# Key and query norms by crossbar DMA and GpSimd sums, shifts of two slots in one instruction, and 32 more score blocks on VectorE, in a one-core attention and GLU kernel

## The chip, the cores and the metric

The kernel runs on one core of one Trainium2 chip. The metric is the device time of one execution in microseconds (us), as a median of several executions. All executions here are of one core, so "state" only means that a run was not more than 1.5% above the fastest of the same kernel; all runs quoted are in the fast state. Beside the time, each run has the mean granted clock of TensorE (1.0 is full speed).

## The reference

A gate mixes an attention block of 32 heads of 16 numbers with a gated linear unit, for 2048 tokens of 512 numbers, all in bf16:

```python
qkv = (x @ wqkv).reshape(B, S, 3, H, Dh).transpose(2, 0, 3, 1, 4)   # S 2048, H 32, Dh 16
q, k, v = qkv[0], qkv[1], qkv[2]
scores = einsum("bhqd,bhkd->bhqk", q, k) * Dh ** -0.5
a = einsum("bhqk,bhkd->bhqd", softmax(scores), v).transpose(...).reshape(B, S, D) @ wo
h = sigmoid(x @ w_gate) * (x @ w_up)          # 512 -> 1792
b = h @ w_down
g = sigmoid((x * gate_w).sum(-1))
out = g * a + (1 - g) * b
```

Every head has 16 x 4 score blocks of 128 keys by 512 queries, 2048 blocks in all, and each of their 134 million scores has to be exponentiated. That is the work that counts here.

## The kernel before

The kernel is a planner and a player. A list of tasks, each with an engine, an expected duration, what it depends on and the buffers it holds, is put in order by a simulated run of the engines; then every engine plays its list. Instructions on an engine run strictly in that order. The numbers of the plan (priorities, and per unit of four heads a set of "knobs") are tuned to the kernel.

The exponentials are shared out. ScalarE takes most blocks, two or three to an instruction. VectorE takes some by integer arithmetic on the bits of an fp16 number: one pass from PSUM makes a block of bits, and two shifted copies (shifts by a constant, within SBUF) are weighted together afterwards by the value matmuls, so such a block costs three value matmuls instead of one. `D_HALVES` says how many pairs of blocks of each of the 32 units go to VectorE; the sum is 267.

```python
# a pair of blocks on VectorE: the pass from PSUM is make_x; two shifts, m = 1 and 2, of 128x1024
for m in range(1, NPH):
    x = P.add("dve", 0.36, lambda v, bp=bp, m=m: v.tensor_scalar(
        PDu[:, bp.slot, m, :, :], PDu[:, bp.slot, 0, :, :], float(PH_OFF[m]), None, op0=ALU.add), [], [bp], kind="x", prio=PH_PRIO)
# blocks on ScalarE, two or three in one instruction
e = P.add("act", 0.175 + 0.3665 * len(ts), lambda a: a.activation(some(PA, out), some(ps_all, bs), ACTF.Exp, bias=ACT_BIAS, scale=SCALE), ...)
```

The softmax is made safe by a bound: minus half the squared norm of each query and minus half the largest squared norm of a key are put into two spare rows of the 32-row score matmul. The norms are made like this for three of the four groups of eight heads and for 15 of the 16 query blocks:

```python
# key_proj(g, c), g > 0: a key block of 128 rows (8 heads) by 512 keys
ev = dve.tensor_copy(kraw, bk(b))                                # from PSUM
s  = pool.tensor_tensor(ksq, kraw, kraw, ALU.mult)               # squares, GpSimd
...                                                              # two masks of the keys, GpSimd tensor_scalar
last = P.group(..., full(b2, wn, ksq))                           # sums of 16 rows: a matmul on TensorE
eNK[g, c] = dve.tensor_reduce(am[:, g, c:c + 1], bk(b2), AX.X, ALU.min)    # VectorE, from PSUM
# query(c, g)
ev = dve.tensor_copy(Q[:, slot, 0, :], bk(b))
s  = pool.tensor_tensor(qsq, Q0, Q0, ALU.mult);  cp = pool.tensor_copy(Q1, Q0)
l2 = P.group(..., full(b2, wn, qsq))                             # TensorE
en = dve.tensor_scalar(nsb, bk(b2), a_[:, g:g + 1], None, op0=ALU.add)     # VectorE, from PSUM
for r in range(2): dma("sp", Q[o:128:32, slot, r, :], nsb[o:128:32, :], ...)
```

## Time and profile before

Median 755.75 us in the three runs taken first (755.69 to 756.17), with the clock at 0.999 in the profiled run.

The table of stretches gives one line for a stretch: its bounds, its length, then the busy us (and count of instructions) of TensorE, of its weight loads, of VectorE, of ScalarE and of GpSimd, then the granted clock, the DMA share and the GB/s.

### The profile page before, as it was taken

How to read it: one execution, taken by the hardware profiler on the slowest of the kernel's cores; microseconds unless marked ns; L12 is line 12 of the kernel's file. 1: busy time of each engine (PE TensorE's matmuls, PEld its weight loads, DVE VectorE, ACT ScalarE, POOL GpSimd, SP SyncE). 2: the span in 40 equal slices, each digit the busy share in tenths (PEclk: the TensorE clock that was granted, in tenths of full speed). 3: DMA queues.
4: the chain of work that ended last, by engine and by line, in shares of the span. 5: the costliest groups of instructions: out<-in, count | busy, mean ns of one | idle time of the engine just before them, and what ended most of it. 6: DMA issues, size and time to landing. Idle time of an engine off the chain costs nothing.

```text
span 754.4 us, 21827 instructions
## 1 busy us (share of the span) xinstructions
PE 739.0 (98%) x9617; PEld 218.0 (29%) x9617; DVE 663.1 (88%) x1311; ACT 734.7 (97%) x822; POOL 111.4 (15%) x198
## 2 busy tenths in 40 slices
PE   8999999999999999999999999999999999999997
PEld 5233232332222222222222222222222222222222
DVE  4999999999898988778899888998889888978986
ACT  5999999999999999999999999999999999999994
POOL 4532625420100101001010010101001000000000
PEclk9999999999999999999999999999999999999999
DMA  9300000040000000000010000000000010000000
GB/s 299 121 10 9 16 4 16 9 115 9 8 9 9 16 16 22 23 2 16 9 17 9 9 23 17 22 9 17 9 1 16 16 23 23 9 10 8 15 2 30
DMA packets 34839, 19.22 MB, mean 25 GB/s; under 512 B 26688, under 2 KB 32696, under 8 KB 34744
## 3 DMA queue, kind: packets, MB, share of 16 engines
q1 hardware_dynamic: 33352, 16.38, 8.4%
q8 instruction: 75, 1.23, 0.7%
q10 hardware_dynamic: 1392, 1.44, 0.6%
q14 instruction: 20, 0.16, 0.1%
HBM read 9.70 MB, written 2.10 MB: 16 GB/s over the span
## 4 chain that ended last, share of the span: by engine, by line
ACT 75%; PE 19%; DVE 4%; DMA 1%; ACTq 0%; issue 0%; DVEq 0%
ACT PA L920 72%; PE ps_all L746 7%; PE ps_all L946 6%; PE ps_all L955 5%; ACT tT L904 3%; DVE PD L928 1%; DVE PD L984 1%; DMA PD<-in_A_x_dram 1%; PE ps_all L749 1%; PE ps_all L866 0%; DVE un L779 0%; DVE am L792 0%; PE ps_all L729 0%; DVE ost L1077 0%; ACTq L635 0%; DVE Q L830 0%
## 5 line engine op out<-in xcount | busy, mean ns | idle before, releaser
L920 ACT ACTIVATE PA<-ps_all 128x1024 bf16<-128x1024 f32 (+1 forms) x744 | 710.5, 1177 | 0.9 <-PE ps_all L946 0.5
L928 DVE TENSOR_SCALAR PD<-ps_all 128x512 uint16<-128x512 f32 x534 | 357.2, 685 | 59.8 <-PE ps_all L946 43.4
L946 PE MATMUL ps_all<-Q,K 32*128 32x512 bf16 x2048 | 301.5, 384 | 6.1 <-ACT PA L920 4.6
L955 PE MATMUL ps_all<-PA,V 128*17 128x512 bf16 x1514 | 242.3, 382 | 1.0 <-ACT PA L920 0.7
L984 DVE TENSOR_SCALAR PD<-PD 128x1024 uint16<-128x1024 uint16 x534 | 216.9, 438 | 4.2
L955 PE MATMUL ps_all<-PD,Vm 128*17 128x512 f16 x1068 | 189.9, 381 | 0.2 <-DVE PD L984 0.2
L946 PEld LDWEIGHTS ps_all<-Q,K 32*128 32x128 bf16 x2048 | 75.0, 91 | 303.5 <-ACT PA L920 272.5
L955 PE MATMUL ps_all<-PD,V 128*17 128x512 f16 x534 | 146.3, 382 | 0.0
L746 PE MATMUL ps_all<-xT,wg 128*32 128x512 bf16 x896 | 74.5, 384 | 0.0
L955 PEld LDWEIGHTS ps_all<-PA,V 128*17 128x17 bf16 x1514 | 55.9, 88 | 55.5 <-issue 43.2
L746 PE MATMUL ps_all<-un,hT 128*32 128x512 bf16 x896 | 71.7, 383 | 0.0
L746 PE MATMUL ps_all<-xT,wu 128*32 128x512 bf16 x896 | 70.0, 383 | 0.1
L1022 POOL TENSOR_TENSOR rs<-rec,e 128x16 f32<-128x16 f32 x32 | 8.3, 259 | 407.3 <-DVE rec L1020 407.3
L955 PEld LDWEIGHTS ps_all<-PD,Vm 128*17 128x17 bf16 x1068 | 44.2, 88 | 34.3 <-issue 26.2
L907 DVE SCALAR_TENSOR_TENSOR hT<-tT,ps_all 128x512 bf16<-128x512 bf16 x56 | 38.1, 680 | 8.6 <-PE ps_all L746 7.6
L904 ACT ACTIVATE tT<-ps_all 128x512 bf16<-128x512 f32 x56 | 42.7, 762 | 0.0
L831 POOL TENSOR_TENSOR qsq<-Q 128x512 bf16<-128x512 bf16 x15 | 16.0, 1069 | 159.7 <-DVE Q L830 159.7
L955 PEld LDWEIGHTS ps_all<-PD,V 128*17 128x17 bf16 x534 | 33.6, 88 | 18.5 <-issue 14.9
L784 POOL TENSOR_SCALAR K<-un,msk 128x512 bf16<-128x512 bf16 x28 | 26.6, 954 | 8.6 <-DVE un L771 5.8
L746 PEld LDWEIGHTS ps_all<-xT,wu 128*32 128x32 bf16 x896 | 19.7, 95 | 26.2 <-issue 13.6
L746 PEld LDWEIGHTS ps_all<-xT,wg 128*32 128x32 bf16 x896 | 17.8, 94 | 26.1 <-issue 20.4
L746 PEld LDWEIGHTS ps_all<-un,hT 128*32 128x32 bf16 x896 | 17.6, 94 | 24.3 <-issue 19.0
(92 smaller groups left out, 331.6 us busy)
## 6 DMA issues: line engine op xcount, KB each, us to landing
wg<-in_B_w_gate_dram SPq DMA_DIRECT2D x1, 1792.0 KB, 11.0
wu<-in_B_w_up_dram SPq DMA_DIRECT2D x1, 1792.0 KB, 14.4
un<-in_B_w_down_dram SPq DMA_DIRECT2D x1, 1792.0 KB, 8.2
out_dram<-ost SPq DMA_DIRECT2D x14, 128.0 KB, 1.8
PD<-in_A_x_dram SPq DMA_DIRECT2D x4, 256.0 KB, 5.6
PD<-in_A_x_dram ACTq DMA_DIRECT2D x4, 256.0 KB, 6.8
un<-in_A_wqkv_dram SPq DMA_DIRECT2D x2, 384.0 KB, 8.8
mid<-mid SPq DMA_TRANSPOSE x45, 2.4
```

The lines of the kernel that those rows point to most:

```text
L746: i = pe.matmul(bk(b)[32 * j:32 * j + 32, :], w()[:, 32 * j:32 * j + 32], x(), start=first, stop=last, tile_position=(0, 32 * j), skip_gro ...
L749: return (MM, lambda pe: pe.matmul(bk(b), w(), x(), start=first, stop=last), four)
L784: eK[g, r, c] = P.add("pool", 1.0, lambda p, r=r: p.tensor_scalar(K[:, g, r, c * 512:(c + 1) * 512], kraw[:, kr.slot, :], msk[:, r:r + 1], ...
L831: s = P.add("pool", 1.15, lambda p: p.tensor_tensor(qsq[:, sq.slot, :], Q[:, bq.slot, 0, :], Q[:, bq.slot, 0, :], ALU.mult), [ev], [sq, bq ...
L904: et = P.add("act", 0.48, lambda a: a.activation(tT[:, t_.slot, :], bk(b), ACTF.Tanh, scale=0.5), [l1], [b, t_], kind="m")
L907: e_h[c, ft] = P.add("dve", 0.62, lambda v: v.scalar_tensor_tensor(hT[:, h_.slot, :], tT[:, t_.slot, :], 1.0, bk(b2), ALU.add, ALU.mult), ...
L920: e = P.add("act", 0.175 + 0.3665 * len(ts), lambda a: a.activation(some(PA, out), some(ps_all, bs), ACTF.Exp, bias=ACT_BIAS, scale=SCALE) ...
L928: return P.add("dve", 0.076 + 0.534 * len(ds), lambda v: v.tensor_scalar(PDu[:, bp.slot, 0, i:i + len(ds), :], some(ps_all, bs), EXP_A, EX ...
L946: return pe.matmul(bk(b), K[32 * j:32 * j + 32, g, r, kt * 128:(kt + 1) * 128], Q[32 * j:32 * j + 32, bq.slot, r, :], start=True, stop=Tru ...
L955: return pe.matmul(bk(bpv)[32 * j:32 * j + DH + 1, :], lhs(h), rhs(), start=t.first, stop=t.last, tile_position=(0, 32 * j), skip_group_ch ...
L984: x = P.add("dve", 0.36, lambda v, bp=bp, m=m: v.tensor_scalar(PDu[:, bp.slot, m, :, :], PDu[:, bp.slot, 0, :, :], float(PH_OFF[m]), None, ...
L1022: e2_ = P.add("pool", 0.2, lambda p: p.tensor_tensor(r4(rs), r4(rec), e2[:, 4 * c:4 * c + 4][:, :, None].to_broadcast([128, 4, 4]), ALU.mu ...
```

## The change

The intent is to take work off ScalarE, the engine that most of the chain consists of, and give it to VectorE, which gets room by losing the norms. Four parts:

1. Norms: each block is transposed by a DMA, squared on GpSimd as before, and summed over its 16 numbers by four GpSimd additions of 256, 128, 64 and 32 columns. Queries are then scaled on GpSimd and transposed back. The norm matmul on TensorE and the VectorE instruction from PSUM go; for keys some small VectorE instructions on 128x32 come.
2. Shifts: when two shifts by the same constant are ready together, one instruction of 128x2048 does both.
3. Blocks: `D_HALVES` sums to 283, so 32 more blocks go from ScalarE to VectorE. A fourth buffer for VectorE's blocks.
4. The plan: a look-ahead to the next unit's value matmuls, new knobs, and more waits between instructions of one engine, with fewer semaphores for DMAs.

```diff
-D_HALVES = (8, 8, 8, 8, 9, 6, 10, 8, 8, 9, 8, 9, 7, 8, 8, 9, 9, 8, 9, 9, 9, 8, 9, 9, 7, 8, 8, 9, 8, 9, 9, 8)
+D_HALVES = (9, 9, 8, 8, 10, 6, 10, 9, 8, 9, 10, 10, 7, 8, 8, 10, 10, 10, 10, 9, 10, 8, 10, 9, 7, 8, 8, 9, 9, 10, 9, 8)
 ... (priorities and knobs: cut)
+        if t.kind == "x" and t.sets:
+            o = next((x for x in self.ready[e] if x.kind == "x" and x.sets and x.n == t.n), None)
+            if o is not None:
+                self.ready[e].remove(o)
+                self._absorb(t, o)
 ... (look-ahead to the next unit's value matmuls: cut)
-        if d.eng == t.eng:
-            if t.eng in ("pe", "sp") or not raw:
+        if d.eng == t.eng:
+            if t.eng in ("pe", "sp"):
                 return
 ...
+    def head_sums(src, deps, bufs):
+        s = Buf(pmid)
+        d = dma_t(lambda: mdt(s), src, deps, bufs + [s])
+        e = pl(1.07, lambda g: g.tensor_tensor(md(s), md(s), md(s), ALU.mult), [d], prio=0.5, bufs=[s])
+        v = lambda: md(s).rearrange("p (x d) -> p x d", d=16)
+        for n in (8, 4, 2, 1):
+            e = pl(0.22 + 0.054 * n, lambda g, n=n: g.tensor_tensor(v()[:, :, 0:n], v()[:, :, 0:n], v()[:, :, n:2 * n], ALU.add), [e],
+                   prio=0.5, bufs=[s])
+        return s, d, e, lambda: v()[:, :, 0]
 ... (keys)
-            s = P.add("pool", 1.15, lambda p: p.tensor_tensor(ksq[:, sq.slot, :], kraw[...], kraw[...], ALU.mult), ...)
+            s, d, e, sums = head_sums(lambda: kraw[:, kr.slot, :], [ev], [kr])
+            if c == 0: eNK[g] = small(lambda v: v.tensor_copy(km[:, :], sums()), ...)
+            else:      eNK[g] = small(lambda v: v.tensor_tensor(km[:, :], km[:, :], sums(), ALU.max), ...)
+            if c == 3: ... (two more maxima, one transpose back, one reduce, one scaling by -0.5)
 ... (queries)
-        l2 = P.group(key - 8.0, [full(b2, lambda: wn[:, :], lambda: qsq[:, sq.slot, :], True, True)], ...)
-        en = P.add("dve", 0.68, lambda v: v.tensor_scalar(nsb[:, ns.slot, :], bk(b2), a_[:, g:g + 1], None, op0=ALU.add), ...)
+        s, d, e, _ = head_sums(lambda: Q[:, bq.slot, 0, :], [ev], [bq])
+        d2 = dma_t(lambda: mdt(s2), lambda: md(s), [e], [s, s2])
+        en = pl(0.95, lambda p: p.tensor_scalar(md(s2), md(s2), -0.5, a2[:, g:g + 1], op0=ALU.mult, op1=ALU.add), ...)
```

## The prediction

> **What bounds the kernel now.** I read the page's engine shares first, then the 40 slices, then the chain that ended last, the groups of instructions, and the waits of ScalarE. From the page (busy time and share of the span; busy tenths per slice; the shares of the chain):
>
> ```profile
> PE 739.0 (98%) x9617; PEld 218.0 (29%) x9617; DVE 663.1 (88%) x1311; ACT 734.7 (97%) x822; POOL 111.4 (15%) x198
> ...
> DVE  4999999999898988778899888998889888978986
> ACT  5999999999999999999999999999999999999994
> POOL 4532625420100101001010010101001000000000
> ...
> ACT 75%; PE 19%; DVE 4%; DMA 1%; ACTq 0%; issue 0%; DVEq 0%
> ```
>
> ScalarE has no open slice between the first and the last, and three quarters of the chain is ScalarE. VectorE has gaps everywhere except in the first third. GpSimd is nearly idle after it. The table of stretches around those borders:
>
> ```profile
> 0.00:20.00 20.00, 17.54 (x161) 10.82 (x161) 10.40 (x27) 11.75 (x20) 10.08 (x35) 1.00 0.95 306
> 20.00:742.00 722.00, 713.28 (x9318) 203.54 (x9316) 646.70 (x1275) 721.11 (x801) 101.06 (x163) 1.00 0.07 17
> 742.00:754.40 12.40, 8.20 (x142) 3.62 (x140) 6.04 (x12) 1.83 (x3) 0.22 (x1) 0.95 0.14 44
> ```
>
> Columns: stretch, its length, then busy us of TensorE, its weight loads, VectorE, ScalarE, GpSimd. In the 722 us of the middle ScalarE is idle for 0.9 us. So the time is 20 us of lead-in, ScalarE's list of work, and a tail of some 12 us that TensorE and VectorE end. TensorE is idle for 8.7 us there by its busy time, VectorE for 75 us. What fills ScalarE and VectorE, from the groups split by shape (count, busy us, mean ns, idle before):
>
> ```profile
> L920 ACT ACTIVATE PA<-ps_all 128x1024 bf16<-128x1024 f32 x718 | 677.9, 1164 | 0.5 <-PE ps_all L946 0.5
> L928 DVE TENSOR_SCALAR PD<-ps_all 128x512 uint16<-128x512 f32 x534 | 357.2, 685 | 59.8 <-PE ps_all L946 43.4 <-PE ps_all L955 13.5
> L984 DVE TENSOR_SCALAR PD<-PD 128x1024 uint16<-128x1024 uint16 x534 | 216.9, 438 | 4.2
> L904 ACT ACTIVATE tT<-ps_all 128x512 bf16<-128x512 f32 x56 | 42.7, 762 | 0.0
> L920 ACT ACTIVATE PA<-ps_all 128x1536 bf16<-128x1536 f32 x26 | 39.2, 1518 | 0.4 <-PE ps_all L955 0.4
> ```
>
> There are 2048 score blocks (128 keys by 512 queries). ScalarE exponentiates 718x2 + 26x3 = 1514 of them. VectorE takes 534 by integer arithmetic: one pass from PSUM per block, and two shifts for each pair of blocks (267 pairs, 534 shifts). A ScalarE duration of 1164 ns overlaps its neighbour; in the merged chain, 86 such instructions take 78.83 us, so **one exp of two blocks costs 0.917 us, 0.458 us per block**.
>
> **What the Trainium skill says.** (1) "Perfetto Trace Analysis", section Identifying the Most-Contended Engine: optimise the engine with the highest occupancy, and do not judge TensorE by matmul busy time. The trace agrees: TensorE shows 98% and ScalarE 97%, yet it is TensorE's weight loads for scores that wait for ScalarE (272.5 us in 645 waits), while ScalarE waits for scores 0.5 us in all. (2) "VectorE: DVE Perf Modes", section The perf-mode tier table: a 16-bit tensor_scalar within SBUF can run at four elements a cycle, one with a PSUM operand at two at most. The shifts agree: two in a row cost 0.73 us against 0.43 for one, so 0.33 us each for 1024 elements, while 512 from PSUM take 0.60. (3) "SBUF — State Buffer", section Who interferes with whom: VectorE in such a two-port mode and GpSimd exclude each other for a whole instruction. The trace agrees in part: around 341.5 us a GpSimd multiply of 1.15 us stretches one shift to 1.26 us from 0.43; but at 70.4 us two shifts beside a GpSimd mask of the keys take 0.78 us together, hardly more than 0.73. (4) "GPSIMD Engine Reference", section Engine selection: sums of two inputs are about twice as slow on GpSimd. The trace shows its 128x512 multiply at 1.04 us; that matters little for an engine busy 15%.
>
> **The change part by part.**
>
> *More blocks on VectorE.* The list of pairs per unit sums to 267 before and 283 after: 16 pairs, 32 blocks, leave ScalarE. ScalarE: 16 exps of two x 0.917 = **-14.7 us**. TensorE: each exp needs a row of score matmuls of 0.32 us and about 0.11 us more to return, read off the timeline at 300 to 302 us (score sets at 300.27 and 301.14 with two other slots of 0.22 between). If the extra VectorE blocks ride in free lanes of the other sets, that is -16 x 0.43 = -6.9 us. Each VectorE block has three value matmuls instead of one: +64 matmuls in four lanes, +16 slots x 0.22 = +3.5. VectorE: +32 x 0.60 + 32 x 0.34 = +30.1 us.
>
> *Norms.* Twelve key blocks (groups 1 to 3) and fifteen query blocks lose their norm matmul, a slot of 0.22 each: 27 x 0.22 = -5.9 us of TensorE, and 27 holdings of a PSUM bank. VectorE loses 12 reduces and 15 additions at about 0.60 to 0.66 net each: -7.2 - 9.9 = -17.1. It gains, per key group, some eight instructions of 0.15 us and one reduce of about 0.25: three groups, +4.5 us. GpSimd keeps its 27 multiplies, and gets 27 trees of four additions (I take 1.7 us each from the kernel's own figures, an estimate) and 15 scalings of 0.95: +60 us, so about 170 of 740. SyncE gets 27 + 15 + 3 more transposes at 1.2 us of issue and 2.4 us to landing; its queue is empty most of the time. A query is ready perhaps 7 us later after its projection (two transposes and the tree for a matmul and an addition), and its key is only a little earlier, but a unit lasts 23 us and four query buffers exist: hidden.
>
> *Two slots in one shift.* A merged shift saves the fixed part of one: 0.33 - 1024/4/0.96 GHz = 0.07 us, an estimate with the rate of page (2). Two shifts of one phase must be ready together. I guess 150 merges: -10 us of VectorE.
>
> *VectorE in sum:* +30.1 - 17.1 + 4.5 - 10 = +7.5. Blocking by the added GpSimd work, an estimate: the shifts lasting over 0.6 us in the trace now lose some 10 us to about 100 us of GpSimd work after 20 us; 60 us more cost +6. So about 677 us busy of some 742, 91%. The first quarter is the tight place: it is 116.75 of 120 us busy at 40 to 160 us, gets 4 of the 16 pairs (+7.5) and 4.5 of small work, and loses 12 reduces and three additions (-9.2).
>
> *TensorE in sum:* -6.9 + 3.5 - 5.9 = **-9.3 us**, against -14.7 for ScalarE. With 8.7 us idle before, it would be left 3 us idle: 99.5% busy. But its packing has slack: single-lane score sets and part-filled value sets exist in the timeline, and the new look-ahead to the next unit's value matmuls can fill some.
>
> *The rest.* All four first key copies move to ScalarE, 2 x 0.49 us more, mostly before the first exp at 19.9 us, where ScalarE still has gaps. VectorE's chain to the first query gets up to 0.6 us shorter. Lead-in: -0.5 to +0.5. The tail is not touched.
>
> So ScalarE's floor is 755.75 - 14.7 = 741.0, plus 0 to 4 us of gaps where TensorE or VectorE falls behind. **I predict 742.5 us.**
>
> **Rivals.** (a) TensorE becomes the bound: by its own saving alone 755.75 - 9.3 = 746.4, minus what packing gives. For it: the 99.5% above. Against it: 645 waits of score weights for ScalarE say that it runs ahead, filling with other work. (b) VectorE becomes the bound in the first quarter through GpSimd blocking, and its late shifts hold back value matmuls and PSUM banks: I give this up to 6 us, about 748. For it: 97% busy there. Against it: a fourth PD buffer and merged shifts relax it. (c) Late queries at the start of a unit: some 3 us at a few boundaries, about 750; against it, query projections are planned units ahead. (d) All goes well, and freed PSUM banks allow more exps of three: a triple adds 1.344 us for three blocks, 0.448 each, so even 30 more save under 1 us; with a shorter lead-in 739 to 740.
>
> **Range and chances.** 738.5 to 748 covers the floor with a good lead-in up to rival (b). Faster by over 2% means under 740.6, just below the floor, so it needs (d): 0.28. Slower by over 2% would need broken overlap: 0.01. Within 2%: 0.71.
>
> **What would show it.** Right: ScalarE again idle under 5 us between first and last exp, some 1482 blocks there, 566 on VectorE; VectorE busy 665 to 690; GpSimd about 170; no line of the removed additions; merged shifts of 128x2048. Rival (a): ScalarE waiting for scores over 5 us in many short waits, evenly spread. Rival (b): these waits in the first quarter, with shifts of 1 us and more there. Rival (c): one wait of several us at a unit's start, behind a DMA. Wrong altogether would be a gain beyond ScalarE's 14.7 us, or longer exps.

## More of the kernel before

Before, from 40 to 140 us:

```profile
40.00:140.00 100.00, 98.29 (x1471) 31.43 (x1472) 97.31 (x192) 99.80 (x109) 41.50 (x60) 1.00 0.06 11
```

The reader should see that three engines are full here at once. ScalarE hardly waits, but VectorE has less than 3 us left in 100. Later in the kernel, when the key and value projections are over, the slices of VectorE in the prediction have gaps again.

## The result, and the profile after

| | median us | range | clock of the runs |
|---|---|---|---|
| before | 755.96 | 755.69 to 756.41 | 0.999 (profiled run) |
| after | 763.26 | 762.67 to 764.83 | 0.991 to 0.996 |

A ratio in this document is the mean time of one kernel's fast runs over that of the other's fast runs of the same rounds, so it is not quite the ratio of the medians quoted. After over before is 1.0099, with a 95% interval of 1.0082 to 1.0117. The change costs 1%, where the prediction had 742.5 us and a range that ended at 748.

From the page of the changed kernel, the engines, the slices of VectorE, ScalarE and GpSimd, and the chain that ended last:

```profile
PE 734.2 (96%) x9587; PEld 218.7 (29%) x9587; DVE 681.3 (89%) x1311; ACT 724.5 (95%) x789; POOL 171.6 (23%) x322
...
DVE  4899999969998899788999999999997788999984
ACT  6988998999999999999999999999999999999994
POOL 5678795402020120212002020022102000000000
...
PE 55%; DVE 22%; ACT 19%; DMA 1%; issue 1%; ACTq 0%; DVEq 0%
```

The totals look like the prediction: GpSimd 171.6 us (predicted 170), VectorE 681.3 (677), and ScalarE 10 us less. But ScalarE has slices of 80% near the start, just where GpSimd's slices read 6, 7, 8, 7, 9, 5, and VectorE's share of the chain rose from 4% to 22%. The stretch from 40 to 140 us of the changed kernel:

```profile
40.00:140.00 100.00, 93.01 (x1542) 32.23 (x1538) 98.71 (x186) 88.92 (x92) 77.07 (x134) 0.98 0.19 35
```

ScalarE lost 10.9 us of 100 against before, VectorE is the full engine at 98.7, and GpSimd almost doubled. What ScalarE waited for, from the table of waits of the changed kernel, first for the stretch from 20 to 145 us, then from 145 to 750 us (us in all, number of waits, longest):

```profile
ACT PA L977 <- PE ps_all L1011: 12.4, 22, 1.2
```

```profile
ACT PA L977 <- PE ps_all L1011: 6.0, 12, 0.9
```

Two thirds of the waits for scores are in the first sixth. Counting score matmuls in the two traces (there are 2048 in each, and times are taken from each span's start) says the same in another way: score matmul 64 starts 2.1 us later than before, number 192 8.5 us later, number 320 (at 129 us before, 143 us after) 13.6 us, number 448 15.4 us. From there the lag stays near 15 us to number 960, and then shrinks to 6.9 us at the last one, as ScalarE's shorter list begins to pay. **Most of the loss is made in the first 145 us.** The chain that ended last runs almost wholly on VectorE from 26 to 137 us.

Why VectorE is slow there is seen in its groups by shape. First before, from 20 to 131 us (the same part of the work), then after, from 20 to 144 us; after the bar stand the busy us and the mean ns of one:

```profile
L984 DVE TENSOR_SCALAR PD<-PD 128x1024 uint16<-128x1024 uint16 x78 | 34.4, 471 | 0.3
```

```profile
L988 DVE TENSOR_SCALAR PD<-PD 128x1024 uint16<-128x1024 uint16 x58 | 34.9, 616 | 0.2
L988 DVE TENSOR_SCALAR PD<-PD 128x2048 uint16<-128x2048 uint16 x13 | 10.8, 829 | 0.0
...
L830 DVE TENSOR_TENSOR km<-km,mid 128x32 bf16<-128x32 bf16 x9 | 3.5, 391 | 0.0
```

A shift of one slot takes 616 ns on average instead of 471. The kind of moment that makes this mean, from the timeline of the changed kernel at 52 us (start, length, engine):

```profile
52.64 1.04 POOL L791 TENSOR_TENSOR mid<-mid 128x512 bf16<-128x512 bf16 x1
52.66 2.38 DVE L988 TENSOR_SCALAR PD<-PD 128x1024 uint16<-128x1024 uint16 x2
53.75 0.73 POOL L794 TENSOR_TENSOR mid<-mid 128x256 bf16<-128x256 bf16 x1
```

This view joins instructions of one line and prints the first one's shape. One by one, the records are a shift of one slot of 1.30 us and a merged shift of two slots of 1.15 us; undisturbed they take about 0.41 and 0.70 us (c2 below). The first ends after the squares of 1.04 us, the second after the addition of 0.73 us. In this stretch GpSimd carries, from its groups between 20 and 144 us, 17 squares (18.2 us) and 68 additions (34.5 us).

Not every GpSimd instruction holds a shift off. I compared recorded starts and lengths of the one-slot shifts with a usual 415 ns, taking those that start at least 60 ns after a GpSimd instruction and 60 ns before its end. In the changed kernel 12 start under squares and are 416 ns late on average, of 548 ns that the squares still had to run; 12 start under the first addition and are 359 ns late, of 489. In the kernel before, 15 start under a mask of the keys; they are late by 1 ns in the median, and it is the masks that are longer, by 292 ns on average over 767 ns. So squares and additions hold shifts off, and masks mostly give way to them.

### The profile page after: what moved, and what is told of

Read it like the earlier page. It is cut to its first block, busy times and chain, and to the rows that moved or that the text cites. A ratio compares the mean times of both kernels' runs of the same rounds, so it can differ in the third digit from the quotient of the medians.

```text
span 761.7 us, 21879 instructions
## 1 busy us (share of the span) xinstructions
PE 734.2 (96%) x9587; PEld 218.7 (29%) x9587; DVE 681.3 (89%) x1311; ACT 724.5 (95%) x789; POOL 171.6 (23%) x322
## 4 chain that ended last, share of the span: by engine, by line
PE 55%; DVE 22%; ACT 19%; DMA 1%; issue 1%; ACTq 0%; DVEq 0%
PE ps_all L775 19%; PE ps_all L1011 19%; ACT PA L977 18%; PE ps_all L1020 16%; DVE PD L993 11%; DVE PD L988 8%; ACT tT L961 1%; DMA PD<-in_A_x_dram 1%; DVE un L822 1%; DVE mid L1067 1%; DVE Q L891 1%; PE ps_all L778 1%; DMA mid<-mid 1%; DVE hT L964 1%; DVE V L936 1%
## 5 line engine op out<-in xcount | busy, mean ns | idle before, releaser
L977 ACT ACTIVATE PA<-ps_all 128x1024 bf16<-128x1024 f32 (+1 forms) x709 | 696.8, 1160 | 19.2 <-PE ps_all L1011 18.4
L993 DVE TENSOR_SCALAR PD<-ps_all 128x512 uint16<-128x512 f32 x566 | 377.0, 681 | 46.7 <-PE ps_all L1011 42.5
L1020 PE MATMUL ps_all<-PA,V 128*17 128x512 bf16 x1482 | 239.0, 383 | 1.6 <-DVE PD L993 1.4
L988 DVE TENSOR_SCALAR PD<-PD 128x1024 uint16<-128x1024 uint16 (+1 forms) x507 | 237.3, 493 | 3.0
L1020 PE MATMUL ps_all<-PD,V 128*17 128x512 f16 x566 | 138.4, 383 | 0.0
L794 POOL TENSOR_TENSOR mid<-mid 128x256 bf16<-128x256 bf16 (+3 forms) x108 | 52.1, 499 | 4.0
L892 POOL COPY Q<-Q 128x512 bf16<-128x512 bf16 x15 | 10.6, 708 | 147.7 <-DVE Q L891 145.9
L961 ACT ACTIVATE tT<-ps_all 128x512 bf16<-128x512 f32 x56 | 40.1, 716 | 0.0
L1020 PEld LDWEIGHTS ps_all<-PD,V 128*17 128x17 bf16 x566 | 31.9, 88 | 19.1 <-issue 15.4
L791 POOL TENSOR_TENSOR mid<-mid 128x512 bf16<-128x512 bf16 x27 | 28.6, 1058 | 13.0 <-DMA mid<-Q 12.5
```

Of the source, the lines that this page charges most:

```text
L791: e = pl(1.07, lambda g: g.tensor_tensor(md(s), md(s), md(s), ALU.mult), [d], prio=0.5, bufs=[s])
L794: e = pl(0.22 + 0.054 * n, lambda g, n=n: g.tensor_tensor(v()[:, :, 0:n], v()[:, :, 0:n], v()[:, :, n:2 * n], ALU.add), [e], prio=0.5, buf ...
L892: cp = P.add("pool", 0.7, lambda p: p.tensor_copy(Q[:, bq.slot, 1, :], Q[:, bq.slot, 0, :]), [ev], [bq], kind="m")
L961: et = P.add("act", 0.48, lambda a: a.activation(tT[:, t_.slot, :], bk(b), ACTF.Tanh, scale=0.5), [l1], [b, t_], kind="m")
L988: return v.tensor_scalar(a[:, :, x.n, :], a[:, :, 0, :], float(PH_OFF[x.n]), None, op0=ALU.add)
L993: return P.add("dve", 0.076 + 0.534 * len(ds), lambda v: v.tensor_scalar(PDu[:, bp.slot, 0, i:i + len(ds), :], some(ps_all, bs), EXP_A, EX ...
```

## The experiments

The theory: the squares and additions on GpSimd hold VectorE's shifts off while they run. In the first 145 us VectorE has no room for it, scores are then not taken out of PSUM in time, TensorE and ScalarE wait behind it, and 14 us are lost. Rivals: (i) the 32 more blocks are simply too many for VectorE; (ii) norms come late through two transposes and a chain of five GpSimd instructions, and units wait for their queries; (iii) merged shifts come late and hold back value matmuls; (iv) the loss is spread over the kernel. One more has to be asked: (v) GpSimd's list is played strictly in order, so the added work may only delay other GpSimd work that somebody waits for.

Rival (ii) falls by the trace alone: for 14 of the 15 queries made in this way, the DMA that writes the last norm row is issued 16 us or more before the first score matmul that reads it (57 us or more for 13 of them); only the first has 4.0 us (issued at 66.0 us, used at 70.0). Rival (v) falls for the changed kernel in the same way: in its table of waits from 20 to 145 us no engine waits for GpSimd, and the longest waits of TensorE's matmuls name VectorE.

All kernels of the table keep the order of instructions of the kernel that they come from on every engine, except the last, so that only the named cost moves. Kernels that leave out the norms still give results within the tolerance, since the bound only matters for large scores; they are experiments, not kernels to use. "40 to 140 us" is that stretch of their profiles. Each ratio is to the runs of before on the same chip, whose medians were 755.96 to 756.23 us; differences between kernels below are differences of medians, in part from different chips.

| kernel | median us | ratio to before, 95% interval | ScalarE in 40 to 140 us | GpSimd there |
|---|---|---|---|---|
| before | 755.96 | 1 | 99.80 | 41.50 |
| after | 763.26 | 1.0099 [1.0082, 1.0117] | 88.92 | 77.07 |
| a1_tiny_trees | 755.77 | 0.9995 [0.9978, 1.0012] | 92.59 | 62.17 |
| b3_before_pool_load | 763.69 | 1.0099 [1.0084, 1.0114] | 97.36 | 60.81 |
| b4_tiny_keys | 759.46 | 1.0037 [1.0012, 1.0062] | 93.08 | 68.47 |
| b5_tiny_queries | 759.10 | 1.0039 [1.0021, 1.0057] | 91.81 | 71.64 |
| b6_split_merged | 769.52 | 1.0179 [1.0163, 1.0194] | 85.00 | 71.90 |
| c1_memset_trees | 759.80 | 1.0047 [1.0002, 1.0092] | 89.98 | 53.17 |
| c3_many_memsets | 766.24 | 1.0129 [1.0114, 1.0145] | 87.62 | 66.60 |
| d3_no_trees | 754.62 | 0.9997 [0.9972, 1.0022] | 94.15 | 51.07 |
| c2_memset_all | 748.70 | 0.9907 [0.9892, 0.9922] | 97.79 | 39.25 |
| t1_replanned | 755.26 | 0.9983 [0.9966, 0.9999] | 96.53 | 77.15 |

### a1_tiny_trees: the additions and scalings made one column wide

```diff
-... g.tensor_tensor(v()[:, :, 0:n], v()[:, :, 0:n], v()[:, :, n:2 * n], ALU.add)
+... g.tensor_tensor(v()[:, 0:1, 0:1], v()[:, 0:1, 0:1], v()[:, 0:1, 1:2], ALU.add)
-... p.tensor_scalar(md(s2), md(s2), -0.5, a2[:, g:g + 1], ...)
+... p.tensor_scalar(md(s2)[:, 0:1], md(s2)[:, 0:1], -0.5, a2[:, g:g + 1], ...)
```

> Same order on every engine as the changed kernel, but the 108 tree additions and 15 scalings on GpSimd touch one column only (results wrong on purpose). Theory lock (GpSimd's added instructions lengthen VectorE's shifts in the first 140 us): 741 to 748 us, shifts that overlap GpSimd back near 0.42 us, ScalarE idle under 4 us. Rival blocks (VectorE simply has too many blocks and small instructions): still 758 to 764. Rival late chain (norms ready too late because the trees take longer): also fast, so this run alone does not tell it from the lock.

755.77 us: 7.5 us of the loss go with the size of these instructions, with every wait and every transpose still there. They are not free when tiny: 68 of them between 20 and 144 us still take 15.8 us of GpSimd, 253 ns each, so this is not yet the kernel without them. The time lies between the 741 to 748 us expected under the theory and the 758 to 764 us of rival (i), so by itself this run shows only that the size of these instructions counts.

### b3_before_pool_load: the kernel before, with the same additions beside it

Nothing of the change is in this kernel. GpSimd only gets, after each block of squares, the four additions, on a scratch buffer that nobody reads, and for the early queries one scaling.

```diff
+        for n in (8, 4, 2, 1):
+            one(lambda p, n=n: p.tensor_tensor(v()[:, :, 0:n], v()[:, :, 0:n], v()[:, :, n:2 * n], ALU.add))
+        if full:
+            one(lambda p: p.tensor_scalar(scr[:, :], scr[:, :], -0.5, 1.0, op0=ALU.mult, op1=ALU.add))
```

> The kernel before with the same order, and after each of its squares on GpSimd four tree additions (and a scaling for queries of the first two chunks) on scratch that nobody waits for, some 45 us of GpSimd. Lock: 760 to 770 us, VectorE's shifts longer in the first 160 us. Late chain: 756 to 758, since no norm waits for the load. Blocks: 756.

763.69 us, +7.5 us, with old blocks, old norms, old waits and single shifts. Work on an engine that was busy 15%, whose results nobody awaits, makes the kernel 1% slower, and none of rivals (i) to (iii) is in it. But it does not show the holding alone. In its profiled run (764.85 us) the shifts from 20 to 144 us are longer (523 ns on average), and score matmul 384 (153 us before) is 3.3 us late; at number 448 the lag is 8.9 us, and it then stays at 8.5. The jump is in one place, and there rival (v) is at work: two loads are queued before value copies that are ready at 153 us, so these start only at 157.8 us, and TensorE waits. From the waits of 145 to 180 us, and the stretch:

```profile
PE ps_all L960 <- POOL Vm L899: 2.2, 1, 2.2
```

```profile
156.00:162.00 6.00, 3.78 (x49) 1.08 (x41) 3.03 (x5) 2.85 (x3) 4.04 (x12) 0.66 0.01 3
```

A dip of the clock to half follows (6.8 us from 157.9 us). It is not the whole of the jump: one of the four runs took 762.72 us at a clock of 0.999. So about 3 us of this run come with longer shifts, and over 5 us with late work of GpSimd itself and the dip behind it.

### b4_tiny_keys and b5_tiny_queries: one kind at a time

```diff
-            s, d, e, sums = head_sums(lambda: kraw[:, kr.slot, :], [ev], [kr])
+            s, d, e, sums = head_sums(lambda: kraw[:, kr.slot, :], [ev], [kr], True)      # b4: tiny; b5: the same for queries, with scalings
```

> Changed kernel, same order, only the 12 key trees made tiny (wrong on purpose), query trees whole. Lock: most of the first quarter's loss goes, 746 to 753 us. Blocks: 758 to 764. If only late queries matter: 760 to 764.

> The changed kernel with the tree additions and scalings of the 15 query blocks made one column wide, those of the 12 key blocks kept, same order. Theory (only the first 145 us count): of the 17 trees in the first 125 us 5 are queries, so 5 of 17 of the gain of making all tiny (763.3 to 755.8): about 2 us, 761, with a spread of 1.5 us where the TensorE clock dips. Rival (the loss is spread over the kernel, where 10 more query trees lie): half or more of the gain, 759.5 or less.

b4 gave 759.46 us, b5 759.10: the two halves gain 3.8 and 4.2 us, near the 7.5 of both. Both expectations missed: b4 was to come to 746 to 753 us under the theory and landed in the range of rival (i), and b5 was to be 761. The five early query blocks of 17 are worth more than 5 of 17, and rival (iv) seems to have a point. Counting score matmuls settles it for the profiled runs: b5 is 3.4 us ahead of the changed kernel at number 320, 5.6 at number 704 and 6.4 at the end. So three of its 6.4 us come after 145 us, and in part they may come from the clock, since that run kept 1.0 where the changed kernel dipped at 247 us. The four runs of b5 spread over 757.23 (clock 1.0) to 760.34 (0.995), which is as large as the question. Both halves count, and the share of the early five is not settled to better than 2 us.

### b6_split_merged: the 59 merged shifts played as two instructions each

```diff
-            at = sorted(b.slot for b in x.sets)
+            at = [v.tensor_scalar(PDu[:, b.slot, x.n, :, :], PDu[:, b.slot, 0, :, :], float(PH_OFF[x.n]), None, op0=ALU.add) for b in x.sets]; return at[-1]
```

> Changed kernel, same order, each of the 59 merged shifts played as two. If merging saves what the prediction estimated (0.07 us each): 763 to 767 us. If a merged shift hurts by holding GpSimd off for longer: 757 to 761.

769.52 us, above both ranges. Merging saves 6.3 us, 0.11 us of kernel time for each of 59, where VectorE is short. Whether merged shifts come late (rival iii) this run does not test, since the two halves still stand in the same place and signal together; c2 below, which keeps the merged shifts and is fast, answers it.

### c1_memset_trees and c2_memset_all: instructions that only write

In c1, each addition and each scaling becomes a one-column memset. In c2, each of the 27 squares does too, so that all GpSimd work on the norms is gone but its order, its transposes and its waits stay.

```diff
-... g.tensor_tensor(v()[:, :, 0:n], v()[:, :, 0:n], v()[:, :, n:2 * n], ALU.add)
+... g.memset(v()[:, 0:1, 0:1], 1.0)
-... p.tensor_scalar(md(s2), md(s2), -0.5, a2[:, g:g + 1], ...)
+... p.memset(md(s2)[:, 0:1], 1.0)
# c2 as well:
-        e = pl(1.07, lambda g: g.tensor_tensor(md(s), md(s), md(s), ALU.mult), [d], ...)
+        e = pl(1.07, lambda g: g.memset(md(s)[:, 0:1], 1.0), [d], ...)
```

> Changed kernel, same order, tree additions and scalings replaced by one-column memsets on GpSimd that read nothing (wrong on purpose; the norms only keep the exponentials in range). Theory lock: VectorE's lengthening in the first 144 us falls from 15 us (after) and 10.5 us (tiny trees) to 5 to 8 us, time 748 to 754 us. If the rest is not from GpSimd: 755 to 757 as with the tiny trees.

> As c1, and the 27 squares are memsets too, so that GpSimd keeps only the key masks, query copies and small work that the kernel before has as well. Lock: lengthening under 4 us as in the kernel before, time 743 to 749 us. If VectorE's blocks alone are too many: over 752 us.

c2 ran in 748.70 us, 14.6 us below the changed kernel and 0.9% below before, at a clock of 1.0 in three of its four runs. All 566 blocks are on VectorE, the shifts are merged, the transposes and their waits are in place: rivals (i) and (iii) are out, and of (ii) the transposes; the chain of additions is shorter here, so for that part the issue times above stand. Its stretch, and its shifts from 20 to 144 us:

```profile
40.00:140.00 100.00, 97.86 (x1739) 34.75 (x1735) 98.99 (x205) 97.79 (x105) 39.25 (x139) 1.00 0.27 49
```

```profile
L988 DVE TENSOR_SCALAR PD<-PD 128x1024 uint16<-128x1024 uint16 x64 | 29.2, 474 | 0.2
L988 DVE TENSOR_SCALAR PD<-PD 128x2048 uint16<-128x2048 uint16 x15 | 10.4, 701 | 0.0
```

Shifts are back at 474 ns, where they were before the change (471), and ScalarE has 97.8 of its 100 us, with VectorE as full as ever: it now does more in the same time (205 instructions against 186). Measured against this run, the changed kernel starts score matmul 320 12.1 us later and the last one 15.2 us later, so four fifths of its loss lie in the first 145 us and one fifth comes later.

c1 disappointed: 759.8 us, above the 748 to 754 us expected, not better than a1, and spread from 755.66 to 763.25. Its four runs line up with the clock: 755.66 at 1.0, 759.5 at 0.992, 760.1 at 0.993 and 763.25 at 0.989, so against the first a lowering of the mean clock by 0.001 goes with 0.5 to 0.7 us (3.8 us over 0.008, 7.6 us over 0.011). The loss has a second stage, which comes below. But c1 also raised the suspicion that a row of memsets is not harmless.

### c3_many_memsets: rows of memsets in place of the additions

```diff
-... g.memset(v()[:, 0:1, 0:1], 1.0)
+... [g.memset(v()[:, i:i + 1, 0:1], 1.0) for i in range({8: 14, 4: 10, 2: 8, 1: 8}[n])][-1]      # scalings: 16
```

> As c1, but each addition and scaling is a run of 8 to 16 one-column memsets, so that GpSimd is busy about as long as in the changed kernel and the norms are ready as late[...]. Lock: within 3 us of c1. Late chain or plain GpSimd time: near the changed kernel, 759 to 764 us.

This was meant to keep GpSimd's time and take only the holding away, so as to test lateness. It failed as a test: 766.24 us, because the memsets hold the shifts off as well. The group of shifts of this kernel from 20 to 144 us:

```profile
L988 DVE TENSOR_SCALAR PD<-PD 128x1024 uint16<-128x1024 uint16 x58 | 38.4, 677 | 0.2
```

The memsets took 23.8 us of GpSimd there, against 34.5 us of additions, so its time was not kept either. The mean of 677 ns is above that of the changed kernel, one shift beside squares and the memsets that follow took 2.28 us, and one at 124.0 us beside memsets alone 1.49 us. On lateness the run says nothing; for it I rely on the issue times and the table of waits given above.

### d3_no_trees: the additions taken out altogether

Since tiny instructions still take GpSimd's time and rows of memsets hold shifts off, the additions are here not replaced but absent; the semaphore step of each is given by the GpSimd instruction before it.

```diff
-            e = pl(0.22 + 0.054 * n, lambda g, n=n: g.tensor_tensor(...ALU.add), [e], prio=0.5, bufs=[s])
+            e = pl(0.22 + 0.054 * n, None, [e], prio=0.5, bufs=[s])
 ... (player)
+                if t.emit is not None:
+                    acts.append([t, 1 if t.val is not None else 0, need])
+                elif t.val is not None:
+                    acts[-1][1] += 1
```

> The changed kernel with the 108 tree additions taken out altogether (not replaced by anything; the semaphore steps of each are given by the GpSimd instruction before it), the 27 squares and the scalings kept, every engine in the order of the changed kernel. Result right only because the norms do no more than steady the softmax. Theory (every added GpSimd instruction with SBUF inputs keeps VectorE's shifts off while it runs, and this costs in the first 145 us): the additions are 34 us of GpSimd in the first 125 us beside 18 us of squares, so about two thirds of the 14.6 us between the changed kernel (763.3) and the one with all of it emptied (748.7) should go: 752 to 755, with GpSimd at 45 to 50 of 100 us at 40 to 140 us and the clock at 0.998 or more. Rival (the additions matter little, the squares and the transposes do): 757 or more.

754.62 us, inside what the theory said (GpSimd at 51.1 us, just over the 45 to 50 written). The additions cost 8.6 us of the 14.6, and the rest (squares, scalings) 5.9. Shifts of one slot from 20 to 144 us are in between too:

```profile
L987 DVE TENSOR_SCALAR PD<-PD 128x1024 uint16<-128x1024 uint16 x62 | 32.8, 546 | 0.2
```

Along the row after, d3, c2 everything moves together: shift 616, 546, 474 ns; ScalarE's waits for scores from 20 to 145 us 12.4, 6.9, 2.7 us; time 763.3, 754.6, 748.7 us.

### The second stage: the clock

Why does TensorE's clock dip after the change, and not before? The stretches of 3.4 us around the first dip of the changed kernel:

```profile
117.80:121.20 3.40, 3.00 (x83) 1.45 (x83) 3.40 (x8) 2.91 (x4) 1.39 (x4) 1.00 0.11 25
121.20:124.60 3.40, 1.99 (x28) 0.57 (x29) 3.40 (x6) 2.34 (x4) 3.10 (x7) 1.00 0.00 0
124.60:128.00 3.40, 3.40 (x30) 0.48 (x22) 3.00 (x7) 2.61 (x3) 1.65 (x5) 0.52 0.19 39
128.00:131.40 3.40, 3.40 (x80) 1.37 (x76) 2.84 (x7) 3.18 (x5) 0.15 (x1) 0.98 0.28 43
```

VectorE is full and GpSimd busy 3.10 of 3.40 us, TensorE is left with 1.99 of 3.40 us of work, and for the next 3.4 us its clock is half (0.52), with 30 matmuls done instead of 80. The same pair of stretches comes once more, at 244.1 to 250.9 us (2.45 of 3.40 busy, then 0.51). Each dip costs half of 3.4 us, 1.7 us of TensorE's time; two are some 3 of the 14.6 us (an estimate from these lines). That a starved TensorE brings the dip is an inference from two places in one trace and from the clocks of the profiled runs of before (0.999) and c2 (1.0); no run sets it apart, and there is a counterexample: from 87.2 to 90.6 us TensorE is busy only 2.34 us of 3.40, and no dip follows. Nor does the second dip point to the holding, since GpSimd is busy only 0.84 us of the 3.40 before it.

### t1_replanned: the same norms, in a plan that knows of the holding

If the loss comes from a plan that believed in undisturbed shifts, a plan that knows better should recover some of it. The planner was told the measured durations of the additions (0.66, 0.43, 0.38 and 0.41 us) and one rule, and its knobs were searched again; it chose 277 pairs.

```diff
+        if t.kind == "x" and t.sets and self.lock > now:
+            t.dur += self.lock - now            # a shift that starts during such an instruction waits for its end
         free = now + t.dur
+        if t.lk:                                # squares, additions, scalings
+            self.lock = free
```

> The changed kernel with the same instructions for norms, shifts and blocks, but with its order of work made anew: the kernel's own planner is told the measured durations of the GpSimd additions, and that a shift which starts while one of them or a scaling runs is longer by the rest of it; its knobs are searched again under that rule (277 pairs of blocks on VectorE instead of 283, 33 in the first four-unit stretches moved about). Theory (the loss is shifts held off in a stretch that was planned as if they were not): the stretch from 40 to 140 us has ScalarE busy again for 93 to 96 us, and the time is 750 to 755, up to 0.8% faster than the kernel before. Rival (a plan cannot help, as GpSimd's order of arrival decides at random who is held off): 758 or more.

755.26 us, just outside the "750 to 755" and 8 us below the changed kernel. Its stretch:

```profile
40.00:140.00 100.00, 96.75 (x1619) 33.35 (x1618) 94.46 (x180) 96.53 (x101) 77.15 (x138) 1.00 0.20 36
```

GpSimd does the same 77 us there, but ScalarE has 96.5 us instead of 88.9. The lag at score matmul 320 is 6.1 us instead of 13.6. The ratio to before is 0.9983, so this version is faster than before by 0.17%, with an interval that only just leaves out 1, and faster than the changed kernel by 8 us. It does not come near c2's 748.7. But more than the order changed: its first five units have 40 pairs on VectorE, against 44 in the changed kernel and 41 before, so VectorE also has less to do where it is tight (94.5 us of the 100). How much comes from the rule, from the new share of blocks or from the new search alone, no run separates.

## Why the prediction was wrong

By the steps of the prediction:

- **ScalarE's floor of 741.0 us.** Right. 1482 blocks stayed on ScalarE and 566 went to VectorE, as foretold. c2, where only GpSimd's norm work is emptied, ran in 748.7 us, and ScalarE waited 6.4 us for scores in it: 741.0 and 6.4 make 747.4. The floor was there to be had within a few us.
- **TensorE -9.3 us.** Right in direction: 739.0 us busy before, 725.9 in c2, thus -13.1. In the changed kernel it shows 734.2; the two stretches of half clock account for some 3 us of the difference, and the rest is open.
- **VectorE's sum of +7.5.** Nearly right, with one term off in both factors: the merges are 59, not 150, and save 0.11 us each, not 0.07, so 6.3 us and not 10. (The 0.33 us for one of two shifts in a row does not follow from the figures beside it: 0.73 less 0.43 is 0.30.) The small instructions for the keys were taken at 0.15 us; the maxima of 128x32 took 0.39 on average.
- **"60 us more cost +6." This step failed**, in size and in place. Its rate came from before, some 10 us of lengthened shifts per 100 us of GpSimd work. But there, 23 us of that work was masks of the keys, which mostly gave way to the shifts. The added work is of another kind, and comes in rows. From 20 to 144 us alone the shifts of after are longer than those of c2 by 58 x 142 ns and 13 x 128 ns, 9.9 us, and the maxima by 0.8 more. (c2 lacks the squares too, but its shifts are as long as those of the kernel before, 474 and 471 ns.) In time, emptying this work was worth 14.6 us (c2), the additions alone 8.6 (d3).
- **The place.** The prediction booked +6 on VectorE's total of 742 us, where it had 75 us of room. Yet it had called the first quarter "the tight place", and its own numbers for it, 116.75 + 7.5 + 4.5 - 9.2, make 119.55 of 120 us, before any blocking (merges not counted). It never did this sum. There was no room there at all, and 17 of the 27 trees lie there: all 12 of the keys, since the units of this stretch need all key groups in turn, and five of the queries.
- **"Held off in part".** The prediction took two shifts of 0.78 us beside a mask at 70.4 us as a sign that the exclusion is partial. For masks that was right; the step from it to squares and additions was not. The timeline of before at 88 us, GpSimd and VectorE, shows a mask again:

```profile
88.44 2.03 POOL L784 TENSOR_SCALAR K<-un,msk 128x512 bf16<-128x512 bf16 x2
88.48 0.75 DVE L984 TENSOR_SCALAR PD<-PD 128x1024 uint16<-128x1024 uint16 x2
```

Here the shifts are undisturbed, and the two masks, 0.77 us for one that is alone, need 2.03 us: GpSimd was the one that waited, on the engine where nobody noticed. "SBUF — State Buffer", section Who interferes with whom, says: "Issue order, not op shape, decides who blocks." The records do not bear this out: the mask starts 0.04 us before the shifts and still waits, and over the whole trace masks gave way where squares and additions held (the counts above). A recorded start need not be the order of issue, so why the kinds differ stays open.

- **Rivals.** (b), VectorE as the bound in the first quarter through blocking, was the right one, with "up to 6 us" for what is up to 14.6. Its marks came as listed: waits of ScalarE in the first quarter, and shifts over 1 us. (a) needed waits evenly spread; they are not. (c), late queries, does not occur.
- **Not foreseen:** two stretches of 3.4 us at half clock, some 3 us by the estimate above; what sets them off is not shown.

## What to carry to other kernels

An idle engine is not free if its work can hold the bound engine off: before moving work to GpSimd, ask which VectorE instructions in that very stretch the new work will hold off, and charge each collision with what is left of the GpSimd instruction; look in the trace for which kinds hold and which give way. Do the sum for the tightest stretch, not for the span: an engine with 75 us of room overall had half a microsecond of room in the 120 us where the new work had to go. Adding the suspected load to the old kernel with nobody waiting for it (b3) is a good test only with its trace beside it: more than half of the loss in its profiled run came at one place, where the load delayed GpSimd's own list. Taking the load out of the new kernel (c2, d3) was the firmer proof.

## What the Trainium skill lacked or had wrong

- "SBUF — State Buffer", section Who interferes with whom: its exclusive lock for a whole instruction agrees with the squares and additions here (a shift of 1.30 us instead of 0.41 at 52.66 us). Its sentence that issue order, and not the shape of the operation, decides who blocks does not fit the records: 15 shifts that started under a mask were late by 1 ns in the median, 12 under squares by 416 ns on average. It also does not say that the recorded length of an instruction on either engine includes its wait for the other (two masks 2.03 us instead of twice 0.77 at 88.44 us), so that a GpSimd group's mean is no cost of its own.
- The same page lacks how short instructions in a row behave: one-column memsets of GpSimd, run in rows, held the shifts off more (677 ns mean) than the additions that they replaced (616 ns), so emptying instructions does not empty their cost.
- "GPSIMD Engine Reference", section 4.1 Engine selection, compares speeds of an operation on one engine and the other. The skill warns elsewhere that the two engines share their way to SBUF, but no page gives what this costs in kernel time: here 8.6 us for 108 small additions.
- "TensorE: Matmul & The Clock Gate", Part 1, gives an idle window of about 3.4 us as what brings the half clock, and tells of short idles that do so too, without a number. Both dips here lasted 3.4 us, as its window says, but TensorE was busy 1.99 and 2.45 of the 3.40 us before them, and 2.34 of 3.40 us at 87.2 us brought none.
